# RWKV-6 recurrence and hard-swish MLP on one core: K and R of every chunk on VectorE, chunk 6's keys turned by DMA, and a new order of all steps

## The chip, the cores and the metric

The kernel runs on one core of a Trainium2 chip. The metric is device microseconds of one execution. A core has five engines that each work through a queue of their own, in order: TensorE (PE; its weight loads are shown as PEld), VectorE (DVE), ScalarE (ACT), GpSimd (POOL) and SyncE (SP), which here issues nearly all DMAs. The engines wait for each other through semaphores. An instruction that waits holds up everything behind it in its queue.

## What is computed

The reference, cut to what matters:

```python
# r, k, v, w: (batch 4, heads 8, seq 768, head_dim 48); u: (8, 48)
for t in range(S):
    cur = einsum('bhd,bhe->bhde', u * k[t], v[t])
    y[t] = einsum('bhd,bhde->bhe', r[t], state + cur)
    state = w[t][..., None] * state + einsum('bhd,bhe->bhde', k[t], v[t])
x = y.transpose(0, 2, 1, 3).reshape(3072, 384)
h = x @ w_in                                # w_in (384, 2048), float64
g = h * clip(h + 3, 0, 6) / 6
out = g @ w_out                             # w_out (2048, 384), float64; out is float32
```

So there are 32 recurrences over 768 tokens, and an MLP on their outputs. The MLP's weights come in as 64-bit floats, and the kernel turns them into 32-bit ones itself.

## The kernel before, in words

**Chunks.** The sequence is cut into chunks of 128 tokens, 24 in all, numbered in the order in which they are handled (two sequences run side by side, so chunk i follows chunk i - 2 of its sequence). Each chunk has two halves of 64 tokens. For a chunk i, these steps exist, each with a name that the plan uses:

- `feat` i loads r, k and w by channel (line 356; for chunk 0 in two parts, the second is the step `later`); `tok` i loads v by token (368); `rkt` i loads r and k by token (373). All three are on SP's queue.
- `back` i is a scan over w from behind, on VectorE (434, with a reciprocal at 438), which gives E; `fore` i is a scan from the front (443), which gives W. `K` i multiplies k by E (454), `R` i multiplies r by W in place (458). `least` i keeps the products of a half (461, ScalarE).
- `own` i forms the u sums, that is, for each token and head the sum of r, k and u. For i < `BY_PE` VectorE multiplies r and k by channel (467) and TensorE sums them with u as weights (`dot` i, 16 small products, 479). For later chunks GpSimd multiplies r, k and u by token (470, 471) and VectorE sums (`sum` i, 487). `diag0`/`diag1` i put the sums on the diagonals of the score matrix A (495, ScalarE).
- `score` i forms K times R (504); `above` i copies the part above the diagonal into A (511, VectorE).
- The keys are needed by token as well. For i < `FLIP` TensorE turns them (520, four transposes) and ScalarE copies them out (528). For i >= `FLIP`, `split` i (ScalarE, 537) parts the 32-bit words of K into 16-bit halves, `flip` i (SP, 542) is a DMA that transposes, and `turned` i (ScalarE, 526) puts the halves together.
- `write` forms the chunk's keys times values (620), `kvs` i copies them out (631, ScalarE), and `decay`, `mid`, `decb` and `state` i bring the state on (550 to 566, VectorE).
- `read` i of the chunks from block 1 on is one step on TensorE: read the state (598), form the scores and the key-value products of chunk i + 1 (504, 620), read the values (607), and, where `FLIP` does not apply, turn the keys of chunk i + 2. So `read` i needs K, R and the turned keys of chunk i + 1. `leave` i copies y into the MLP's input (706, ScalarE), and `move` (713, SP) moves the last pair of heads to its place by small DMAs, two times two for a block of four chunks.

**The MLP.** Four chunks make a block (512 tokens), six in all. Block 0's up products (739) are plain, 16 steps of 128 columns (f = 0 to 15), each in two or three parts by chunk (`up0.f.c`), each followed by `ramp` (729, ScalarE) and `gate` (750, VectorE). From block 1 on the up products go by a fast matrix scheme with fewer multiplications (840; 40 steps of four matmul records for a block), with sums of weights ahead (`sin`, 787 to 791, VectorE), sums of x (`tx`, the same lines), and reads of the products (848, 855, 857) before `clip` (861) and `gate` (865). The down products (897; `down` block.half.k.x, eight matmul records each) go by such a scheme too, with sums of g (`sum` block.half.k.x, 882) and of w_out (`sout`, 816).

**The weights.** 16 pieces `fetch` 0 to 15 of 768 KB come in through three buffers (397). Each is converted by ScalarE (`low`, 406, and `sign`, 411) and VectorE (`shift`, 417, and `full`, 421). Later 22 pieces come in once more to be vetted (`refetch`, `vet`, 934 to 952).

**What sets the order.** Every step is entered in a plan with its engine, an estimate of its time, what it follows and which buffers it holds. `Plan.order` (line 191) takes the order itself from a string written out by hand, `ORDER` (82 to 115): two characters give the rank of each step. Each engine's queue is that order, restricted to its steps. The plan's estimates set no order; they only say where TensorE gets dummy products in the first 60 us (`Plan.emit`, 232; `spin`, line 1276), which keep it at work while it has nothing else.

The lines that choose by chunk are few:

```python
448        def early(i):
449            return nc.vector if i < EARLY else nc.gpsimd
454            early(i).tensor_mul(d["K"], d["k"], d["E"][:, :, 1:])
458            early(i).tensor_mul(d["R"], d["r"], d["R"])
465            if i < BY_PE:
531            return i >= FLIP
```

Buffers that matter below: three of `feat` (a load waits until K and R, and with `BY_PE` also `own`, of the chunk three before are done), two of K, two of W, one of `rk` (shared by the u products and the split keys), one of `kvs` (shared by the flipped keys and the copied key-value products), four banks for products.

Of the kernel before, what the change touches and what calls it, by code (L numbers as in the profile page):

```python
# [79 lines left out]

CODE = "ABCDEFGHIJKLMNOPQRSTUVWXYZabcdefghijklmnopqrstuvwxyz0123456789+/"
ORDER = (
    "AEAIAHASATAVAKANAOAPAQARAbAjAXAYAZAaAhApAdAoAyA4A7AGALAeAmAiAsAlAWAcAtAuAvA+BCAwAxA8A9BDBPBHBIBMBdBiAfBhA1BKBNBQA6A2"
    "BEBFBJBpBzB0BLBVBnB1CBCJCLCNCeCkAgBYBTBlB7CKBfBRBoBtB4CaChCnB+CACSCWCMCpCrDYC3C5DTDBBjCOBwCsCqCtB3ByCHCfDJDLDUDfC7DD"
    "DRD0D3EDEIEPEVEzB5EUC6DMDaDgDIDADPDXEEEWEcDcD1EoEKFBFJFaFTFwHZG5CgFSDvECEvExD4ELElEyFPFQFhEhFmFWFrF0F/GmG1EXGUEmFiGD"
    "GRFZFbFjFlFvGHGtGFGMGbGpG9HBHFHKHcHdHfHxFRGfGSGZGzG7GYFnF4F9G6HeHtGkGlGoH9HSH/IBIgI1JqFUHMFVGjGuHjH5GnIXIoI+I/JBG4HY"
    "H7JcJsJtJuJvKkK4LELKHaKaJKH+JUJYKSJNJMJQKBKHLMJfKAKOKlKgKnKvLSLiHbK6HiJZKXK8LGJ5KbKuKzLILXK0K+LHLhLNLtLuLyL2MOL9IUJ+"
    "KeKyLYLkLqLBLmLnLsMBMCLeLfLgMdMeMfMuNQLCL7MRLzMFL5L/L1MjMmMxMyMzMGMUMYM7NCNDNwN3PyPvLdNTL8MpM+M6NZM0MqMrNLNkN5NNNRNn"
    "ONNqOQObOxO+PcM/NEN0NMNWNzOCNPOHOUPDPOPbNXN2OAPaO7PdPfPhPjQDQMQKNSOpOeNxOGPHPNN6PMPsP+P/QCO0PCPERWQ+RXRlRvRyScN1Q0PI"
    "PiP4QAQzP1QyQ3RPRQR2QBQIQnR5RFR7R8SQS/TmUBUCPlRxPwQiQxSASzQsRMRbTCTDTGSBSTSpTfS5TiTjTqT4UMQ4SISKRJSlTPTSRVSnSqTWTXUJ"  # L90
    "S7TITdUGTLUOUSUVUZUaUdUeSVTyTZTATsUDUPTNT+UXUoUpU3TtT6UAVQVRVZVaVdVoWuUQU6URUcUuUrVjUsUmUtUxVsVvU4U5VMVzVbV2WQWhW/Xe"
    "YMX1U0WXVHVIVkWPW+VKVlV7WNWfXFWZWzW0XZWGXbXrX3YJU7VrXaWHW2XTXhWkXfXmXpX2X7XHXOXYX+XMYBYCYWYeYxYjBgAFAJAkAnAqAzBWCTCU"
    "BcCbAMA0A5ArA/BXBZBmBrB2A3BABBBOBUCPCwCxCoDFAAABADACAUBkBvCEB6CRDrD7EOEQEaDCDlDnDwDyETEfEiEkE2E8E9FEE/FFFDFLFMFHFXB8"
    "CdDdC/DiD+EdEeEZErC+DWDjDmD/BSBaBbDpDtDxDqDzD2BGBeBsCCCcCiFAFOFgCjClCuDQDVDZEbEpEwC1C2C8CvCyCzEAEHEJCDCVCZE+FGFIDHDK"
    "DOESEYEnCXCYCmDsD5D6EMENERD9EFEGBqBuBxFpFuGLB/CFCQF7F8GODSDeDhEtE3E4DuD8EBEqEuE0B9CGCIEgEjEsDbDkDoE5E6E7C0C4DEGNGXGc"
    "C9DGDNGdGiGxFeFyF3GPGTGsG8G+HDHEHIHNHOHPHRHTHUHhHkHqHrHzH3H6IAIHIIILIPIeIhIiIkInIrI2I3I4I5I6I7JAFdFfFkFqGVGgF2GBE1GA"
    "FzF+FYGCF1GKFCFKFsFtFcFoF5F6GGGQGIGJGhGqFNFxGEGWGeGaG2HXIEGrHLG/HQGyHgHJHlGwG0GvHAHHHmHGHVHuHvHoHpH0H1G3HCHWHnHwHsH8"
    "IVINHyH2H4IJIKIbIpIyJSIZIlIxICISIsIDIMIYIGITIcIvIwI9IRIdIjIFIqIaImIuIQIOJEI8IWItIfIzI0JHJVJgJhJ0J7JGJXKiKjJkJ6LTLUJC"
    "JDJLJPJFJTJnJ1KKJpJxKCJaJbJ2JJJWJmJRJeJzJ/J4KGJIJlJoJOJrJwJyJ9JiJdKDKLJjKIJ3KJKFKPKQKRKUKhKoKVKWLDLWKEKMKtK/KNKTKsLA"
    "J8K3KfK1KcKdKwK9KZKmKYKpKrLFKxK2LQLRLLLOLZLaKqK5K7LJLvLPLrOfL+LVL4LwL6LjMELxMJLbLlLcLpMHMML3MAMIMNMKMLMbMhLoL0MDMPMa"  # L100
    "MVMkNAOgMQMSMcM8MlMvM3NJNgM5NFNcM4NaNlMTMiMsMWMgMwNGNKNdMtM2NfMZNIM1M9NHMnMXNUNeMoNmNBNbNVNhNjNuOIOLOYNoNyOMOnNYNiPr"
    "PtNONpPJPVN/OFOTOjOvOEOROlODOJOqNsN4N8NrN9OPOdOXOoOBOOOZNtOcOKOWOaN7NvOkOmN+OwOSOhOiOyOzO3O4PnPoOuO2PqP2OtO1PKPkOrOs"
    "P0P5OVO6PFPRO8PBPLPeO5O/O9PGPPPTPQPSPWPgPYPZPxPzPAPUPXP8PpPmQVT7TJP3QUQGQYP6QLQJQpP7P9QFQHQOQRQPQQQlQqQWQXQjQkQNQTQS"
    "QeQ5QhQmQ6SJQZQaQbQcQuQ/RERSRhRCRHRUR+R/ShQdQvQ8QfQwRBRLRGRYQ2RASSQtRRQ9RKRNQ1QgRTRaQ7SoRDRZRORgRqR3SDSCSYRdRkTHTURo"
    "RpTQTRRsR4TnTvRmRzR9SOSgSLSRSmStSuS0RfRnR1RcRtR0SUSPSaRuR6SyRiSNSFSGSZRrReSWSrRwS+SMSbSXSfSjSkSxT2T5S1S2TkTrSiSsTxTz"
    "SdSeTYTgSESHS9TOS3TMTBThSwS4SvS6TTTVTETFTbTuTcTeT3T9S8TKTaTlT1TpT/W7X0TwT0UNUhULUWUYUiUEUFUIUUUTUjUfUgUwU1UlUnUyUzUH"
    "UbUkUqU+UvU/VqWyU8U9VSVpVBVVVhVxWFWdWeWwVNVOVWVAVEVGVCVUVeVuVtV5VLVXVTVDVwVPVgWmVFVJWBWxVYVcVfV4V1V6WbXPXQWJWiX5X6Vn"
    "V3WaWcWIWKXqXyViV0V9WEWYW3XIXAXBXdWTWWWsV8WDWRVyWAWVWnWqW4WCWUWjV/WlWSWpXUWMV+XGXiWOWtWgWoWrW8XkXoYHXCXEYKYXW1W9YDYE"
    "XJXKYIYQWvW5YOYVYYY/YZYkYlYqYPYgYUYiYsYtYoYpZAZCYuYvY7Y9YhY5YrY4ZMY6ZEaFZxW6XVXcXwXLXsXgX4XRXSXWXXXnYFXtXuX8X9YRYSYa"
    "YbXjXlXvYGYmYTYfYwZwZTaEYzY0Y1Y2ZGZPZeZlZzZZZbZkaiala+Y3ZHZNY8ZJZQZiZhZnZKZSa2ZDZfZOZcZdZIZFZrZqZLbYZWZjZmZuZ0Z5aLau"  # L110
    "bAZ8aVbdbfaPaUbQbSZgZ1bHbPZRZ2aIaQagaHaOaXaxa5bRZyZ7Z6ZoaKaRafaYakZaZ4bDZ3aJZ+aNaSZ/Z9aTacaMbbaWahaZanaparasbmbnaeaj"
    "bcbpaoaqa3a/aaabbGbLadazawbEatbFbBbOaya4ama7a8bMa9bCbZbgbVbWbhbia6bUbKbTb8bXbtcEb9cDbubjbobsb+brbybxb1bkbqblbwb2b4bz"
    "b0cAcBb5b/cIcKbvb7b3b6cHcCcMcGcJcFcNQoQrZVZXToUKZpaAYyZBXNYAZUZYX/YcXzYNRIRjPuQEZsaBYnY+aDavT8U2YLYdaCa0ZtZvaGa1VmWL"
    "bIbJXDXxbNbabecL"
)
# [1509 lines left out]
```

## Time and profile before

| | |
|---|---|
| three runs | 526.06, 528.02, 531.23 us; median 528.02 |
| the profiled execution | 528.87 us, of which the span from the first to the last instruction is 527.1 us |
| mean granted TensorE clock | 0.997 |
| ScalarE busy | 290.1 us of the span (55%) |
| K and R on GpSimd (lines 454, 458) | 17 each, 25.0 and 25.3 us busy |
| u products on GpSimd (470, 471) | 15 each, 17.5 and 16.5 us busy |
| TensorE's largest lines | 897 (down) and 840 (up), 29% and 28% of the chain that ended last |
| HBM traffic | 59.69 MB read, 4.72 MB written |

A row of the busy groups names the line, the engine, the operation, what is written from what, and the shapes; then comes the count, the busy time in us, the mean of one in ns, and the idle time of the engine just before, with what ended it. A row of the timeline starts with the start and the time of a run of equal instructions. A row of the chain has only start, time and what. TensorE's instructions overlap in the records: a row's time includes the drain of its last one.

### The profile page before, as it was taken

The page shows a single profiled execution, that of the slowest core. Times are in us where ns is not written, and L with a number is a line of the kernel's source. Part 1 is how long each engine was busy: PE and PEld are TensorE (multiplying, and loading weights), DVE is VectorE, ACT ScalarE, POOL GpSimd, SP SyncE. Part 2 cuts the span into 40 slices and gives each one's busy share as a digit, 9 for nine tenths or more (in the row PEclk, how much of TensorE's full clock was granted, in tenths as well). Part 3 has the DMA queues.
Part 4 walks back from the last instruction along what each step waited for, and adds up shares of the span by engine and source line. Part 5 has one row for each costly group of instructions (what it writes and reads, how often), then busy time and mean ns, then how long its engine had stood idle before and what let it go on. Part 6 is the DMA issues. An engine that isn't in the chain of part 4 may idle for free.

```text
span 527.1 us, 13608 instructions
## 1 busy us (share of the span) xinstructions
PE 517.7 (98%) x5642; PEld 477.7 (91%) x5642; DVE 431.6 (82%) x762; ACT 290.1 (55%) x680; POOL 86.7 (16%) x79
## 2 busy tenths in 40 slices
...
GB/s 329 329 275 182 234 285 92 49 53 181 150 3 63 54 172 68 96 206 72 109 99 101 150 10 130 140 101 106 265 33 153 101 151 203 131 199 136 60 10 57
DMA packets 37235, 70.33 MB, mean 133 GB/s; under 512 B 19088, under 2 KB 27184, under 8 KB 37168
## 3 DMA queue, kind: packets, MB, share of 16 engines
...
q14 instruction: 21, 0.17, 0.1%
q10 hardware_dynamic: 128, 0.00, 0.0%
HBM read 59.69 MB, written 4.72 MB: 122 GB/s over the span
## 4 chain that ended last, share of the span: by engine, by line
PE 86%; DVE 6%; DMA 3%; SPq 2%; ACT 1%; issue 1%; DVEq 0%
PE bank L897 29%; PE bank L840 28%; PE bank L739 8%; PE bankS L897 5%; PE bankS L840 5%; PE y_ps L598 2%; PE bank L504 2%; PE y_ps L607 2%; PE y_ps L620 2%; DMA feat_in<-in_feat_dram 1%; PE bankS L1276 1%; PE ps L479 1%; DMA bits<-in_moe_w_in_dram 1%; SPq L713 1%; DVE E L434 1%
## 5 line engine op out<-in xcount | busy, mean ns | idle before, releaser
L861 ACT ACTIVATE clip<-g,three 128x512 f32<-128x512 f32 x80 | 56.1, 719 | 49.0 <-DVE g L857 27.8
L857 DVE TENSOR_TENSOR g<-bank,g 128x512 f32<-128x512 f32 x80 | 53.4, 684 | 26.2 <-PE bank L840 23.1
L897 PE MATMUL bank<-w_out,g 128*128 128x192 f32 x384 | 67.3, 327 | 0.0
L897 PEld LDWEIGHTS bank<-w_out,g 128*128 128x128 f32 x384 | 63.2, 190 | 0.5
L865 DVE SCALAR_TENSOR_TENSOR g<-clip,g 128x512 f32<-128x512 f32 x80 | 59.1, 754 | 4.0 <-ACT clip L861 3.9
L495 ACT ACTIVATE A<-eyes,dg 128x64 f32<-128x64 f32 x192 | 49.8, 338 | 0.5 <-DVE dg L487 0.3
L454 POOL TENSOR_TENSOR K<-feat_in,E 112x512 f32<-112x512 f32 x17 | 25.0, 1469 | 146.0 <-DVE E L434 82.8
L855 ACT COPY g<-bank 128x512 f32<-128x512 f32 x50 | 28.8, 585 | 33.5 <-PE bank L840 32.3
L739 PE MATMUL bank<-xT,w_in 128*128 128x256 f32 (+1 forms) x216 | 46.7, 366 | 0.0
L739 PEld LDWEIGHTS bank<-xT,w_in 128*128 128x128 f32 x216 | 37.4, 194 | 4.5 <-issue 0.3
L458 POOL TENSOR_TENSOR W<-feat_in,W 112x512 f32<-112x512 f32 x17 | 25.3, 1490 | 94.4 <-DVE W L443 80.9
L840 PE MATMUL bank<-xT,w_in 128*128 128x256 f32 x160 | 40.1, 379 | 0.0
L706 ACT COPY xT<-y_ps 48x256 f32<-48x256 f32 x88 | 32.2, 365 | 10.4 <-PE y_ps L607 9.6
L915 ACT ACTIVATE o<-bank 128x192 f32<-128x192 f32 x36 | 11.5, 327 | 47.1 <-PE bank L897 47.0
L897 PE MATMUL bankS<-w_out,g 128*128 128x192 f32 x192 | 34.9, 328 | 0.0
L897 PE MATMUL bank<-more,g 128*128 128x192 f32 x192 | 34.4, 329 | 0.1
L840 PEld LDWEIGHTS bank<-xT,w_in 128*128 128x128 f32 x160 | 30.2, 190 | 3.8
L897 PEld LDWEIGHTS bank<-more,g 128*128 128x128 f32 x192 | 31.4, 190 | 1.1 <-DVE o L917 0.5
L434 DVE TENSOR_TENSOR_SCAN E<-feat_in,back 112x520 f32<-112x520 f32 x24 | 29.9, 1245 | 2.8 <-DMA feat_in<-in_feat_dram 2.8
L470 POOL TENSOR_TENSOR rk<-rk_in 128x384 f32<-128x384 f32 x15 | 17.5, 1164 | 88.9 <-DMA kvs<-rk 39.4
L897 PEld LDWEIGHTS bankS<-w_out,g 128*128 128x128 f32 x192 | 31.6, 190 | 0.2
L840 PE MATMUL bank<-xT,bits 128*128 128x256 f32 x120 | 30.7, 380 | 0.8 <-DMA xT<-xT 0.8
...
## 6 DMA issues: line engine op xcount, KB each, us to landing
feat_in<-in_feat_dram SPq DMA_DIRECT2D x23, 772.5 KB, 5.7
bits<-in_moe_w_in_dram SPq DMA_DIRECT2D x8, 768.0 KB, 7.3
bits<-in_moe_w_out_dram SPq DMA_DIRECT2D x8, 768.0 KB, 5.6
feat_in<-in_moe_w_in_dram SPq DMA_DIRECT2D x8, 768.0 KB, 4.8
feat_in<-in_moe_w_out_dram SPq DMA_DIRECT2D x8, 768.0 KB, 4.5
...
feat_in<-in_wflat_dram SPq DMA_DIRECT2D x6, 768.0 KB, 4.7
```

What stands on the lines that cost most here:

```text
L434: nc.vector.tensor_tensor_scan(out=E_[:, ::-1], data0=d["w"][:, :0:-1], data1=back.rearrange("q p t -> q (p t)")[:, ::-1], initial=0.0, op ...
L454: early(i).tensor_mul(d["K"], d["k"], d["E"][:, :, 1:])
L458: early(i).tensor_mul(d["R"], d["r"], d["R"])
L495: nc.scalar.activation(out=d["A"][:, h, :], in_=eyes, func=ACT.Copy, scale=d["dg"][:, h])
L706: nc.scalar.copy(out=blocks[bk]["xT"][g * GP:g * GP + D, :, at:at + HL], in_=st[i]["y_ps"][a][(g ^ a) * GP:(g ^ a) * GP + D, :, :])
L739: nc.tensor.matmul(h_ps[:, :(c1 - c0) * L], lhsT=w_in[:, f // 2, j, f % 2, :], rhs=b["xT"][:, j, c0 * L:c1 * L], start=(j == 0), stop=(j = ...
L840: nc.tensor.matmul(b["p", d, c][:, z * HB:(z + 1) * HB], lhsT=weight(W_PLACE[r], d)[:, z, :], rhs=x_at(bk, X_PLACE[r]), start=fresh and z ...
L855: nc.scalar.copy(out=out_, in_=src)
L857: nc.vector.tensor_tensor(out=out_, in0=src, in1=out_of(bk, d, other), op=ALU.add if sign > 0 else ALU.subtract)
L861: nc.scalar.activation(out=c, in_=out_of(bk, d, u), func=ACT.Relu, bias=three, scale=twice)
L865: nc.vector.scalar_tensor_tensor(out=g, in0=blocks[bk]["r", d, u], scalar=6.0, in1=g, op0=ALU.min, op1=ALU.mult)
L897: nc.tensor.matmul(b["d", p, to][:, :h], lhsT=a, rhs=w(), start=(f == 0 and k in (1, 5)), stop=(f == HF - 1 and k in (2, 3, 4)), skip_grou ...
```

## The change

Three constants and the order string change; no function does.

```diff
-BY_PE = 9
-FLIP = 7
+BY_PE = 8
+FLIP = 6
 OWN = -16.106
 SOLO = (0, 1, 2, 3, 4)
-EARLY = 7
+EARLY = 24
...
 ORDER = (
-    "AEAIAHASATAVAKANAOAPAQARAbAjAXAYAZAaAhApAdAoAyA4A7AGALAeAmAiAsAlAWAcAtAuAvA+BCAwAxA8A9BDBPBHBIBMBdBiAfBhA1BKBNBQA6A2"
+    "AAAKABAHAIAUAEAFAGAMANAOAWAfAPAQAXAcAgAqAnAsA0A6BFADAiAVAhAeApAZARASAYAaAmAxAzAkAuAyA7A8BQBGBHBKBXBYALA5AwBCBABLA/Aj"
...
```

- `EARLY` 24: `K` and `R` of chunks 7 to 23, 34 steps, are formed by VectorE and no longer by GpSimd.
- `BY_PE` 8: chunk 8's u sums are formed as those of the later chunks. `dot8` (TensorE) goes, `own8` moves from VectorE to GpSimd, `sum8` from ScalarE to VectorE, and the load `rkt8` comes. GpSimd is left with the u products of chunks 8 to 23.
- `FLIP` 6: chunk 6's keys are turned by DMA. The four transposes in `read4` go, `split6` (ScalarE) and `flip6` (SP) come, and `turned6` becomes the longer copy.
- All 1808 steps (1806 before) stand in a new order.

Read out, the order begins so on SP's queue (before, then after):

```
fetch6 feat0 later feat1 tok0 fetch0 tok1 fetch2 feat2 feat3 fetch4 fetch1 fetch3 tok3 u tok2 feat4 fetch7 feat5
feat0 later feat1 fetch1 tok0 feat2 fetch3 tok1 fetch0 feat3 tok3 tok2 fetch2 fetch6 feat4 fetch7 feat5
```

On TensorE at the start:

```
dot0 turn0 kv0 score0 dot1 clear0 first0 turn1 read0 kv1 score1 dot2 up0.1.0 clear1 first1 turn2 up0.0.0 read1 kv2 dot3 up0.8.0 score2
dot0 turn0 dot1 score0 kv0 turn1 clear0 first0 score1 kv1 dot2 read0 clear1 first1 turn2 read1 score2 dot3 kv2 up0.0.0 up0.1.1 turn3
```

On VectorE at the start:

```
shift6 back0 own0 K0 fore0 full6 R0 own1 back1 decb0 fore1 above0 K1 state0 shift0 shift2 R1 full0 back2
back0 own0 K0 fore0 own1 R0 back1 shift1 fore1 above0 decb0 K1 own2 R1 state0 full1 shift3 back2
```

On ScalarE, the conversions (`low` and `sign`) ahead of `leave1` are those of pieces 6, 0, 2 and 4, with `low3`, before, and of 1, 3 and 0 after.

On TensorE between chunk 4's read and chunk 5's, after: `up0.3.0 dot6 up0.11.0 up0.2.0 up0.9.2 up0.11.2 up0.14.2 up0.3.2 dot7 up0.15.2 up0.13.2 up0.7.2 up0.2.2 up0.6.2`.

On TensorE from chunk 6's read to block 1:

```
read6 down0.0.4.1 down0.1.5.0 down0.1.1.0 down0.1.1.1 down0.1.5.1 down0.1.6.0 down0.1.2.0 down0.1.6.1 read7 down0.1.2.1 down0.1.7.0 down0.1.7.1 down0.1.3.0 down0.1.3.1 down0.1.4.0 down0.1.4.1 up1.0.12 up1.0.1
read6 down0.0.4.0 down0.0.4.1 down0.1.5.0 down0.1.5.1 read7 down0.1.6.0 down0.1.6.1 down0.1.2.1 down0.1.7.0 down0.1.7.1 down0.1.3.0 down0.1.3.1 down0.1.4.0 down0.1.4.1 up1.0.1 up1.0.12
```

Ahead of `read6` stand, after: `down0.0.3.0 down0.0.3.1 down0.0.7.0 down0.0.7.1 down0.1.2.0`; VectorE has `out0.0.c12 R7 K8 sum0.1.1.0 out0.0.c22 sout4.0` in that stretch, the first of which follows `down0.0.3.1`.

On SP around chunk 7's way out:

```
flip9 move1.0.0 feat10 feat11 move1.1.0 rkt11 move1.1.1 store0.1 store0.3
move1.0.0 feat9 store0.1 feat10 feat11 move1.1.0 move1.1.1 flip9 store0.2
```

(`move1.0` is block 1's first pair of chunks, 4 and 5; `move1.1` its second, 6 and 7.)

More of the change, by code (lines that the diff above doesn't have):

```diff
@@ L112 @@
-    "bcbpaoaqa3a/aaabbGbLadazawbEatbFbBbOaya4ama7a8bMa9bCbZbgbVbWbhbia6bUbKbTb8bXbtcEb9cDbubjbobsb+brbybxb1bkbqblbwb2b4bz"
-    "b0cAcBb5b/cIcKbvb7b3b6cHcCcMcGcJcFcNQoQrZVZXToUKZpaAYyZBXNYAZUZYX/YcXzYNRIRjPuQEZsaBYnY+aDavT8U2YLYdaCa0ZtZvaGa1VmWL"
-    "bIbJXDXxbNbabecL"
+    "AAAKABAHAIAUAEAFAGAMANAOAWAfAPAQAXAcAgAqAnAsA0A6BFADAiAVAhAeApAZARASAYAaAmAxAzAkAuAyA7A8BQBGBHBKBXBYALA5AwBCBABLA/Aj"
+    "A2A9BDBUBaBhBJBVBdBnBBBoBsB6CZCgA3A4BEBgCGCUBWBZBbBfB1CLCcClBmB0B7CHB4ChCnDSCrC7DeDgBPDECACVC9DbCKB3CFCJC1DODcDpC0C+"
```

58 lines of the change are left out of this document (30 added, 28 removed).

## The prediction, made before the changed kernel ran

> **What bounds the kernel now.** I read the page's totals first, then the chain that ended last, then the busy time by stretches of 30 us.
>
> ```profile
> span 527.1 us, 13608 instructions
> PE 517.7 (98%) x5642; PEld 477.7 (91%) x5642; DVE 431.6 (82%) x762; ACT 290.1 (55%) x680; POOL 86.7 (16%) x79
> PE 86%; DVE 6%; DMA 3%; SPq 2%; ACT 1%; issue 1%; DVEq 0%
> 0.00:30.00 30.00, 26.42 (x440) 24.59 (x440) 25.90 (x47) 21.99 (x58) 3.01 (x15) 1.00 0.87 330
> 60.00:90.00 30.00, 30.00 (x416) 26.34 (x416) 29.45 (x59) 24.93 (x57) 1.18 (x1) 1.00 0.66 227
> 90.00:120.00 30.00, 30.00 (x305) 28.55 (x304) 29.07 (x52) 15.00 (x39) 5.65 (x4) 1.00 0.19 47
> 150.00:180.00 30.00, 30.00 (x376) 27.34 (x371) 29.14 (x53) 20.55 (x45) 5.57 (x4) 1.00 0.14 36
> 270.00:300.00 30.00, 30.00 (x294) 28.92 (x293) 20.37 (x39) 11.88 (x31) 6.75 (x6) 1.00 0.29 82
> ```
>
> A stretch shows its length, then PE, PEld, DVE, ACT, POOL, the clock, DMA share and GB/s. TensorE is busy throughout and makes 86% of the last chain; GpSimd makes none of it. So the relief of GpSimd is worth nothing by itself: only less TensorE work, or an earlier or less broken supply of it, moves the end. VectorE is the second engine, nearly full in 60 to 120 and 150 to 180, with room later (20.37 of 30). Where does TensorE still lose time? In two places.
>
> The first is the start. TensorE is filled there with dummy products (line 1276), and real work waits for data.
>
> ```profile
> L1276 PE MATMUL bankS<-ident 128*128 128x128 f32 x94 | 15.6, 328 | 1.4 <-POOL ident masks.py:199 1.4
> 9.99 2.02 PE bankS L1276 x18
> 5.66 0.56 DVE L417 TENSOR_SCALAR top<-bits 128x768 int32<-128x768 int32 x1 [2.30 <-DMA bits<-in_moe_w_in_dram]
> 6.21 1.24 DVE L434 TENSOR_TENSOR_SCAN E<-feat_in,back 112x520 f32<-112x520 f32 x1
> 33.03 1.24 DVE L434 TENSOR_TENSOR_SCAN E<-feat_in,back 112x520 f32<-112x520 f32 x1 [2.19 <-DMA feat_in<-in_feat_dram]
> ```
>
> 18 dummies in 2.02 us are 0.112 us each, so 94 fill 10.5 us. The scan at 33.03 is chunk 4's and waits 2.19 us for its load: the start is fed by a DMA stream that runs flat out (330 GB/s over 0 to 30).
>
> The second is the step from block 0 to block 1.
>
> ```profile
> 122.42 1.51 ACT L706 COPY xT<-y_ps 48x256 f32<-48x256 f32 x4 [1.64 <-PE y_ps L607]
> 124.58 1.79 SPq L713 DMA_DIRECT2D xT<-xT  x3
> 126.41 0.58 SPq L373 DMA_DIRECT2D rk_in<-in_tok_dram  x1
> 127.10 1.77 SPq L713 DMA_DIRECT2D xT<-xT  x3
> 128.92 2.76 PE L897 MATMUL bank<-more,g 128*128 128x192 f32 x16
> 132.52 1.10 PE L840 MATMUL bank<-xT,bits 128*128 128x256 f32 x4 [0.84 <-DMA xT<-xT]
> 132.83 0.43 DVE L787 SCALAR_TENSOR_TENSOR T__1844<-xT 128x256 f32<-128x256 f32 x1 [3.36 <-DMA out_dram<-o]
> 134.78 1.10 PE L840 MATMUL bank<-T__1844,bits 128*128 128x256 f32 x4 [1.16 <-DVE T__1844 L787]
> 91.23 2.60 PE bank L897 x16
> 161.57 5.18 PE bank L840 x24
> ```
>
> Chunk 7's output is copied out until 123.93, its moves land only at about 132.5, and the x sums start at 132.83. Sixteen down products take 2.60 us in the chain (0.1625 each, 1.30 for a step of eight, which I call a half), so those of 128.92 are issued by 131.5; the first up product starts at 132.52, and the second at 134.78, where 0.86 after the first would do (24 in 5.18 us, 0.216 each, four to a step). That is 1.0 + 1.4 = 2.4 us lost.
>
> **The change part by part.** *K and R of chunks 7 to 23 on VectorE.* 34 instructions leave GpSimd and join VectorE's queue.
>
> ```profile
> L454 POOL TENSOR_TENSOR K<-feat_in,E x17: 1172/1627/1711, 73.6 to 393.4; 112x512 f32<-112x512 f32 x17
> L454 DVE TENSOR_TENSOR K<-feat_in,E x7: 682/685/687, 8.2 to 66.0; 112x512 f32<-112x512 f32 x7
> 109.17 1.40 DVE L791 TENSOR_TENSOR bits<-w_in 128x256 f32<-128x256 f32 x1
> 113.36 0.40 DVE L791 TENSOR_TENSOR bits<-w_in,bits 128x256 f32<-128x256 f32 x1
> L857 DVE TENSOR_TENSOR g<-bank,g 128x512 f32<-128x512 f32 x80 | 53.4, 684 | 26.2 <-PE bank L840 23.1
> L865 DVE SCALAR_TENSOR_TENSOR g<-clip,g 128x512 f32<-128x512 f32 x80 | 59.1, 754 | 4.0 <-ACT clip L861 3.9
> ```
>
> VectorE takes on 34 x 0.685 = 23.3 us. It gives up a stretch: the sum at 109.17, beside a K on GpSimd, took 1.40 instead of 0.40, and the gate of line 865 (both inputs in SBUF) means 754 ns against 684 for the read of line 857, of the same size with one input in PSUM. From the gates alone that is 80 x 0.07 = 5.6 us, which includes GpSimd's u products; at most it is 34 x 1.0. Adding over all VectorE groups what an instruction took beyond its group's median gives 21 us, of which about 16 lie under a K or R. Net load on VectorE: +7, between -11 and +23. On the path I take 0: TensorE's queue has its next products ready in these stretches. If that cover goes, it costs rival two.
>
> *Chunk 8's u sum to GpSimd, chunk 6's keys by DMA.* TensorE loses 16 + 4 instructions.
>
> ```profile
> 40.26 0.56 PE ps L479 x16
> 36.60 0.39 PE ps L520 x4
> L537 ACT COPY rk<-K 112x1024 uint16<-112x1024 uint16 x17 | 17.7, 1040 | 2.0 <-POOL K L454 1.9
> DMA to landing us min/median/max: 2.9/3.1/4.6
> L526 ACT COPY kn<-kvs 128x896 uint16<-128x896 uint16 x17 | 20.4, 1198 | 9.2 <-DMA kvs<-rk 9.2
> ```
>
> That is 0.56 + 0.39, and all of it is on the path: -0.95 us. SP gets one more load (rkt8) and one more flip, ScalarE a split and a longer copy; the split, the flip's 3.1 to landing (the quoted row is that of line 542, the flip) and the copy are 5.3 us behind K6. Between chunk 4's read and chunk 5's, which needs the turned key, the new order has twelve up steps (ten of six 256-wide products at 0.216, 1.3 us; two half as wide) and two u dots of 0.56, some 15 us, so it is hidden (without that cover: up to 5.3).
>
> The Trainium skill speaks against this edit: "VectorE: DVE Perf Modes", section "The three transpose paths", gives TensorE 390 ns and the DMA path 1309 ns for one 128x128 tile. The rows here agree on the order (0.39 us for four tiles against 3.1 to landing). By that rule the edit would add latency, up to +5.3; by the chain, where only TensorE's time counts, it saves 0.39.
>
> *The new order, at the start.* SP's list now begins with chunk 0's and 1's loads and puts five weight pieces ahead of chunk 4's, not six.
>
> ```profile
> feat_in<-in_feat_dram SPq DMA_DIRECT2D x23, 772.5 KB, 5.7
> bits<-in_moe_w_in_dram SPq DMA_DIRECT2D x8, 768.0 KB, 7.3
> L411 ACT ACTIVATE more<-bits 128x768 bf16<-128x768 int32 x16 | 17.1, 1071 | 0.0
> L406 ACT ACTIVATE more<-bits 128x768 uint16<-128x768 uint32 x16 | 17.2, 1077 | 3.8 <-DMA bits<-in_moe_w_in_dram 3.1 <-DVE w_out L421 0.7
> ```
>
> 768 KB less ahead of chunk 4 (the 16 pieces are alike) are 0.786 MB, or 2.4 us at 330 GB/s. On ScalarE one weight conversion (1.077 + 1.071 = 2.15 us) fewer stands ahead of chunk 1's way out (three where there were four), and the first scan need not follow a weight piece (back0 at 6.21 waited behind 5.66 + 0.56; up to 0.7). Against it, chunk 1's turn on TensorE now stands ahead of chunk 0's read and waits for K1, which VectorE forms only after chunk 0's mask copy: about 0.6 later there. Three ways of looking give 0 (if the three weight buffers hold SP's queue, whose later pieces wait for conversions), 2.15 and 2.4. I take -2.2. The bounds: -4.5, if a fair part of the 10.5 us of dummies goes; +1.5, if chunk 0's detour is not made up.
>
> The granted clock rides on this stretch too: six products took 2.59 us at 31.89 where six take 1.46 at 89.77.
>
> ```profile
> 31.89 2.59 PE L739 MATMUL bank<-xT,w_in 128*128 128x256 f32 x6
> 89.77 1.46 PE L739 MATMUL bank<-xT,w_in 128*128 128x256 f32 x6
> ```
>
> That is 1.1 us. The Trainium skill, "TensorE: Matmul & The Clock Gate", Part 1, has the clock fall after an idle window of about 3.4 us that runs free of the program; by it this 1.1 us may go or stay whatever the order, so the sum counts nothing where the row alone would let me take it.
>
> *The new order, at block 1.* Two down halves move from ahead of chunk 7's read to behind it: nine (11.7 us at 1.30) now cover the way from that read to the first up product, where there were seven. In SP's list no load stands between the four moves any more, where rk_in stood with 0.58. That would erase the 2.4. But chunk 7's read now comes four halves (5.2 us) after chunk 6's, where it came after eight. It needs chunk 8's turned key and chunk 7's state: from K8, which VectorE forms three down steps ahead of chunk 6's read, split 1.04, flip 3.1 to 4.6, copy 1.2 and chunk 6's way out (as chunk 7's, 1.5) make 6.8 to 8.3 us, against seven halves, 9.1, and the read between them. So it is just hidden, and a late K8 shows at once. I take -1.8, from -2.4 to +2.
>
> *Everything else.* The later reads are moved by a few products each way; between two of them stand seven halves or as much in up steps, 9.1 us, or more. Nothing there is idle to be won; small new waits may come: +0.5, from 0 to 4.
>
> Sum: -0.95 - 2.2 - 1.8 + 0.5 = -4.45. The profiled execution took 528.87 (its span 527.1 and 1.77 around it), so 524.4. It lies 0.85 above the median of the three runs, 528.02; on their scale, 523.5.
>
> **The rivals.** *One: the start gains more.* If TensorE gets its first long run of products as much earlier as chunk 4's load arrives (2.4) and part of the dummies beyond (4.5 in all), and block 1's 2.4 goes whole: -0.95 - 4.5 - 2.4 = -7.85, and on the scale of the median 520.2. For it: the start is the one place with real slack; against: only three weight pieces can lie unconverted, and ScalarE is at 21.99 of 30 already.
>
> *Two: slower, VectorE becomes the bound.* Place: the in-order queue of VectorE in each of the five blocks from chunk 5's read on. Price: 23.3 us joins it, and only the 5.6 that the gates show comes back; 17.7, of which the stretches with room take a half, leave 9, with TensorE's -0.95 and the start's -2.2 some +6: 534. It decides as soon as a block's stretch has less than some 4 us of 30 free; 60 to 120 and 150 to 180 have under 1. Against it: most other stretches are like 270 to 300, and the stretched sums show that much more than 5.6 comes back.
>
> *Three: nothing but a trade.* Block 1's wait moves to chunk 7's read (a flip of 4.6 or a late K8: +2 in place of -1.8), and the start gives 0: -0.95 + 2 + 0.5 = +1.55, 529.6. For it: the 5.2 us between two reads, the shortest of either order; against: K8 no longer takes GpSimd's 1.6 us.
>
> **How the numbers follow.** My forecast, a gain of 2 to 6.5 us, 0.60; rival one 0.17; rival three 0.15; rival two 0.08. One per cent is 5.28 us, about what a measurement of this kernel tells from no change. Of the forecast's cases nearly half lie beyond it (0.25 of 0.60), and all of rival one's: faster 0.42. Rival two gives slower, 0.08; the rest, 0.50, lies within. The forecast's own range is 521.5 to 526; with rival one and half of rival three, 519 to 528.5.
>
> **What would show it right or wrong.** Right: GpSimd at about 35 us busy (86.7 less 34 at 1.6, and one more u product pair) with only lines 470 and 471 at work; VectorE at 430 to 445 with line 865 back at about 700 ns; chunk 4's scan at about 30 instead of 33.03, and fewer than 94 dummies or an earlier end of them; no wait at block 1's first up products; TensorE's stretches from 150 on as full as before. Wrong: a stall of 2 us or more in front of chunk 7's read (line 598, near 120); line 454 or 458 as releaser of TensorE; VectorE over 29 of 30 in several stretches beyond 180; six 256-wide products of line 739 not seen before 31.89.

## The result, and the profile after

The changed kernel took 521.65 us (median of six runs, 521.15 to 523.82), the kernel before beside it 527.43 (six runs, 526.06 to 531.23). The ratio is 0.9872, with a 95% interval of 0.9844 to 0.99: faster by 1.3%. The profiled execution took 522.23, its span 6.7 us less than before.

The page of the changed kernel: totals, engines, the chain, and two groups of instructions.

```profile
span 520.4 us, 13521 instructions
...
PE 511.6 (98%) x5608; PEld 474.1 (91%) x5608; DVE 434.8 (84%) x796; ACT 292.5 (56%) x680; POOL 39.4 (8%) x47
...
PE 91%; DMA 3%; DVE 2%; ACT 1%; SPq 1%; issue 1%; DVEq 0%
...
L865 DVE SCALAR_TENSOR_TENSOR g<-clip,g 128x512 f32<-128x512 f32 x80 | 53.5, 684 | 6.6 <-ACT clip L861 6.4
...
L470 POOL TENSOR_TENSOR rk<-rk_in 128x384 f32<-128x384 f32 x16 | 19.0, 1187 | 361.4 <-DMA kvs<-rk 111.8
```

TensorE has a larger share of the chain (91% for 86%), VectorE a smaller one (2% for 6%). GpSimd has lost 47 us, and line 865 takes 684 ns where it took 754. VectorE took on 23.3 us of K and R and is busy only 3.2 us longer: its instructions beyond their groups' medians summed to 21.3 us before and to 3.0 now.

By stretches of 30 us (length, then PE, PEld, DVE, ACT, POOL, clock, DMA share, GB/s):

```profile
0.00:30.00 30.00, 27.56 (x493) 25.44 (x494) 26.94 (x51) 22.14 (x62) 3.01 (x15) 1.00 0.90 341
...
60.00:90.00 30.00, 30.00 (x420) 26.82 (x420) 28.19 (x58) 25.51 (x57) 2.00 (x2) 1.00 0.47 156
90.00:120.00 30.00, 29.36 (x413) 28.53 (x412) 29.03 (x58) 14.23 (x39) 0.00 (x0) 1.00 0.38 115
```

VectorE is still nearly full from 60 to 120 (28.19 and 29.03 of 30). The timeline at the start shows chunk 0's scan, chunk 0's read, chunk 1's read, chunk 3's scan and chunk 4's scan:

```profile
3.90 1.24 DVE L434 TENSOR_TENSOR_SCAN E<-feat_in,back 112x520 f32<-112x520 f32 x1 [0.53 <-DMA feat_in<-in_feat_dram]
...
15.43 0.65 PE L598 MATMUL y_ps<-W,S 48*48 48x64 f32 x16
...
20.65 0.65 PE L598 MATMUL bank<-W,S 48*48 48x64 f32 x16
...
21.35 1.24 DVE L434 TENSOR_TENSOR_SCAN E<-feat_in,back 112x520 f32<-112x520 f32 x1
...
32.90 1.24 DVE L434 TENSOR_TENSOR_SCAN E<-feat_in,back 112x520 f32<-112x520 f32 x1
```

The same of before, where the forecast did not show them:

```profile
16.12 0.65 PE L598 MATMUL y_ps<-W,S 48*48 48x64 f32 x16
...
24.35 0.65 PE L598 MATMUL bank<-W,S 48*48 48x64 f32 x16
...
26.60 1.23 DVE L434 TENSOR_TENSOR_SCAN E<-feat_in,back 112x520 f32<-112x520 f32 x1
```

The first scan comes 2.3 us earlier (3.90 for 6.21), chunk 3's 5.25, chunk 1's read 3.7. Chunk 4's scan is where it was (32.90 for 33.03), now with no wait for its load. And at the step to block 1:

```profile
113.05 0.67 PE L598 MATMUL y_ps<-W,S 48*48 48x64 f32 x32 [0.64 <-ACT xT L706]
...
116.30 4.05 SPq L713 DMA_DIRECT2D xT<-xT  x6
...
123.08 0.42 DVE L787 SCALAR_TENSOR_TENSOR T__1814<-xT 128x256 f32<-128x256 f32 x1 [0.49 <-DMA xT<-xT]
...
126.83 1.03 PE L840 MATMUL bank<-T__1814,bits 128*128 128x256 f32 x4
```

No wait stands at the first up products any more; chunk 7's read waits 0.64 us for chunk 6's way out.

To say where the time went, I set against each moment the real TensorE work issued until then: dummies count nothing, an up product of line 840 its 0.216 us, a down product its 0.1625, a 128-wide product of line 739 0.112, the small ones of reads and u sums 0.007 to 0.03, each an issue interval from an undisturbed row. Time passed less this work is **lost TensorE time**. For the two kernels, and for five of the experiments below:

| us lost by | 60 | 100 | 110 | 120 | 140 | 200 | 300 | 515 |
|---|---|---|---|---|---|---|---|---|
| before | 27.1 | 29.9 | 30.8 | 31.0 | 34.5 | 37.8 | 41.9 | 49.3 |
| after | 23.2 | 25.7 | 26.4 | 28.1 | 28.0 | 31.6 | 35.9 | 43.6 |
| K and R alone | 27.1 | 29.7 | 30.6 | 30.8 | 33.2 | 38.5 | 45.4 | 58.2 |
| new order to chunk 8's read | 23.4 | 25.7 | 26.6 | 27.5 | 27.3 | 31.2 | 35.0 | 42.1 |
| new start alone | 21.6 | 25.3 | 32.2 | 32.5 | 33.8 | 37.4 | 41.3 | 48.3 |
| new start, seam mended | 24.5 | 28.6 | 31.6 | 33.1 | 36.4 | 39.2 | 43.9 | 50.9 |
| before, moves first | 27.6 | 30.5 | 31.1 | 31.5 | 32.3 | 35.9 | 40.2 | 47.6 |

The gain of after: 3.9 us up to 60, 0.5 from 60 to 110 (3.2 lost for 3.7), 2.1 from 110 to 140 (1.6 for 3.7); 0.8 is lost again behind that (15.6 for 14.8), and the work itself is 0.8 smaller (473.7 for 474.5). That makes 6.5 of the span's 6.7.

### The profile page after: what moved, and what is told of

Its sections match the earlier page's. It is cut to its first block, busy times and chain, and to the rows that moved or that the text cites. A ratio compares the mean times of both kernels' runs of the same rounds, so it can differ in the third digit from the quotient of the medians.

```text
span 520.4 us, 13521 instructions
## 1 busy us (share of the span) xinstructions
PE 511.6 (98%) x5608; PEld 474.1 (91%) x5608; DVE 434.8 (84%) x796; ACT 292.5 (56%) x680; POOL 39.4 (8%) x47
## 4 chain that ended last, share of the span: by engine, by line
PE 91%; DMA 3%; DVE 2%; ACT 1%; SPq 1%; issue 1%; DVEq 0%
PE bank L897 33%; PE bank L840 28%; PE bank L739 8%; PE bankS L840 5%; PE bankS L897 5%; PE y_ps L598 3%; DMA xT<-xT 2%; PE y_ps L607 2%; PE bank L504 2%; PE y_ps L620 2%; SPq L713 1%; PE bankS L1276 1%; PE ps L479 1%; ACT xT L706 1%; DMA feat_in<-in_feat_dram 1%
## 5 line engine op out<-in xcount | busy, mean ns | idle before, releaser
L861 ACT ACTIVATE clip<-g,three 128x512 f32<-128x512 f32 x80 | 56.4, 719 | 33.8 <-DVE g L857 25.8
L865 DVE SCALAR_TENSOR_TENSOR g<-clip,g 128x512 f32<-128x512 f32 x80 | 53.5, 684 | 6.6 <-ACT clip L861 6.4
L739 PE MATMUL bank<-xT,w_in 128*128 128x256 f32 (+1 forms) x216 | 45.2, 361 | 1.2 <-DMA xT<-xT 1.2
L470 POOL TENSOR_TENSOR rk<-rk_in 128x384 f32<-128x384 f32 x16 | 19.0, 1187 | 361.4 <-DMA kvs<-rk 111.8
L855 ACT COPY g<-bank 128x512 f32<-128x512 f32 x50 | 28.2, 586 | 28.3 <-PE bank L840 25.5
L897 PE MATMUL bank<-more,g 128*128 128x192 f32 x192 | 34.5, 328 | 0.5 <-DVE o L917 0.5
L897 PEld LDWEIGHTS bank<-more,g 128*128 128x128 f32 x192 | 31.6, 190 | 1.1 <-DVE o L917 0.7
L526 ACT COPY kn<-kvs 128x896 uint16<-128x896 uint16 x18 | 21.6, 1201 | 15.8 <-DMA kvs<-rk 7.8
L443 DVE TENSOR_TENSOR_SCAN W<-feat_in,start 112x520 f32<-112x520 f32 x24 | 29.6, 1233 | 0.0
```

The costliest lines, as they stand in the source:

```text
L443: nc.vector.tensor_tensor_scan(out=W_, data0=d["w"][:, :-1], data1=starts[i % 2].rearrange("q p t -> q (p t)"), initial=0.0, op0=ALU.mult, ...
L526: nc.scalar.copy(out=d["kn"].bitcast(U16).rearrange("q p (d two) -> q two p d", two=2), in_=d["flip"])
L739: nc.tensor.matmul(h_ps[:, :(c1 - c0) * L], lhsT=w_in[:, f // 2, j, f % 2, :], rhs=b["xT"][:, j, c0 * L:c1 * L], start=(j == 0), stop=(j = ...
L855: nc.scalar.copy(out=out_, in_=src)
L861: nc.scalar.activation(out=c, in_=out_of(bk, d, u), func=ACT.Relu, bias=three, scale=twice)
L865: nc.vector.scalar_tensor_tensor(out=g, in0=blocks[bk]["r", d, u], scalar=6.0, in1=g, op0=ALU.min, op1=ALU.mult)
```

## The experiments

Each ratio is against the kernel before, run beside it on the same chip, with its 95% interval. The experiments ran on two chips at four times, and the kernel before took 527.98 to 528.73 us beside them (527.43 beside the changed kernel), so differences of a microsecond between two variants are not settled by their times alone.

### K and R on VectorE, by themselves

In the order of before (first), and taken out of the changed kernel (second):

```diff
-EARLY = 7      # K and R alone: the kernel before, and only this
+EARLY = 24
```
```diff
-EARLY = 24     # the changed kernel with K and R on GpSimd
+EARLY = 7
```

> The kernel before with one constant changed: K and R of chunks 7 to 23 on VectorE, the old order kept. Theory A (TensorE bounds; the gain lies in the order, at the start and at block 1): K and R on VectorE are worth nothing by themselves, 526.5 to 528.5 beside 527.4 of before. Theory B (K and R off GpSimd are the gain: no stretched sums, no wait for GpSimd): 524 or less, at least 3 us of the 5.8. Theory C (VectorE overloaded in 60 to 120 where it stood at 29 of 30 us): 529 or more, with new waits before line 598 or 840.

> The changed kernel with K and R of chunks 7 to 23 back on GpSimd, the new order kept. Theory A: the start and its 4 us stay, chunk 7's read waits some 1 to 2 us more for K8 and R8; 522 to 524.5. Theory B: the gain goes, 526 or more. If the order is made for K and R on VectorE (the two belong together): VectorE's queue waits for GpSimd in many places, over 527.

K and R alone: **536.19** against 527.98, 1.0173 [1.0136, 1.0209], slower by 8.2 us. The changed kernel with K and R on GpSimd: **521.61**, 0.9881 [0.9857, 0.9906], the changed kernel's own time, and a little under the 522 at which its expectation began. So the edit is worth nothing in the new order and costs 1.7% in the old one. The page of the second kernel shows GpSimd at work again, at no cost in time:

```profile
PE 514.0 (99%) x5608; PEld 476.1 (92%) x5608; DVE 430.4 (83%) x762; ACT 292.7 (56%) x680; POOL 89.1 (17%) x81
...
L865 DVE SCALAR_TENSOR_TENSOR g<-clip,g 128x512 f32<-128x512 f32 x80 | 57.1, 730 | 5.1 <-ACT clip L861 4.9
```

GpSimd is busy 89.1 us, line 865 is stretched to 730 ns, and the time is the same. K and R alone has the sign of theory C, but not its place. Its loss is not VectorE's load (438.2 us, 82% of its span; the changed kernel has 434.8, 84%, and no loss) but the order of VectorE's queue. The timeline near 412, at its longest wait:

```profile
411.91 0.68 DVE L865 SCALAR_TENSOR_TENSOR g<-clip,g 128x512 f32<-128x512 f32 x1
412.51 0.69 DVE L458 TENSOR_TENSOR W<-feat_in,W 112x512 f32<-112x512 f32 x1
...
413.34 0.69 PE L504 MATMUL bank<-W,K 48*64 48x64 f32 x32 [2.15 <-DVE W L458]
```

R stands at a place that was planned for GpSimd, where it had no gates ahead of it (there it ran at 397.80 in the kernel before); here it comes behind them, and TensorE waits 2.15 us for R. Its clock falls behind that, as the stretches of this kernel show:

```profile
411.00:414.50 3.50, 1.35 (x87) 1.25 (x81) 3.22 (x7) 2.87 (x4) 0.00 (x0) 1.00 0.19 19
414.50:418.00 3.50, 3.50 (x32) 2.79 (x22) 3.46 (x8) 0.05 (x1) 0.00 (x0) 0.53 1.37 245
```

Until 140 us this kernel is no worse than before (33.2 lost for 34.5); it loses from 180 on. The other waits there are shorter, 0.2 to 0.8 us each, for results of VectorE (lines 550, 787, 857, 917) and of ScalarE (526, 706, 915).

### Where in the order the gain lies

The steps are kept; two orders are joined at a read. K and R of chunks 7 to 23 are on GpSimd in both of these.

```diff
 order of the steps:
-as changed
+as before up to chunk 8's read, then as changed        (later part alone; BY_PE 9, FLIP 7)
+as changed up to chunk 8's read, then as before        (new order to chunk 8's read; BY_PE 8, FLIP 6)
```

> All constants as before; the old order up to chunk 8's read, the new order after it, K and R on GpSimd. By the theory that the gain ends with block 1's start: 527 to 528.5, as before. If the later blocks have a share: 526 or less.

> As the start-only kernel, but with the new order kept up to chunk 8's read, past block 1's start. If block 1's step gives 1.6 net beside the start: 521 to 522, as the changed kernel, and 1 to 2 us under the start-only kernel. If the step gives nothing net (its 2.4 us went to chunk 7's read): the same as the start-only kernel.

The later part alone: **529.04** against 528.08, 1.0023 [1.0, 1.0046]. The new order up to chunk 8's read: **521.03**, 0.9863 [0.9833, 0.9893]. All of the gain lies ahead of 140 us; the order of the four later blocks is worth nothing, and so is K and R on VectorE there.

Two earlier tries at this cut had K and R on VectorE in the old part too, or chunk 6's turn at a place of my choice in it, and both lost more than they were to show:

```diff
+as changed up to chunk 5's read, then as before        (EARLY 24)
+as before up to chunk 8's read, then as changed        (EARLY 24, BY_PE 8, FLIP 6)
```

> The three constants of the change; the new order up to chunk 5's read, the old one for all steps after it. Theory A, by the lost TensorE time added up in both profiles (27.0 us against 23.0 at 60 us): the start alone gives 4.0, and TensorE's 20 fewer products 0.7: 522.5 to 524, with block 1's wait of about 2 us still there. If the rest of the order made the gain instead: 526 or more.

> The three constants of the change; the old order up to chunk 8's read, the new one for all steps after it. Theory A: nothing is won behind block 1's start, so what stays is TensorE's 0.7: 526 to 527.5. If the new order of the later blocks has a share: 525 or less.

**535.35** and **537.22** against 527.98, 1.0155 [1.0124, 1.0187] and 1.0192 [1.0156, 1.0228]. The first has the loss of K and R alone in its old part, and near 105 us that of the new start alone, shown below. The second is a case of its own: chunk 6's turned key came to stand on ScalarE ahead of the activations of the up products.

```profile
81.29 1.19 ACT L526 COPY kn<-kvs 128x896 uint16<-128x896 uint16 x1 [3.10 <-DMA kvs<-rk]
...
84.22 6.95 PE L739 MATMUL bank<-xT,w_in 128*128 128x256 f32 x18 [5.62 <-DVE g L750]
```

ScalarE waits 3.10 us for the DMA's transpose, and TensorE 5.62 for what is queued behind it; TensorE's clock is 0.51 from 83.0 to 90.0. This is the price of this edit without its cover. The forecast gave it as up to 5.3, which the wait alone exceeds, and left the clock out. It says nothing against the changed order, which has the cover, and neither run divides the gain.

### The start

One weight piece first again, as in the order of before (SP's load, with its conversions on ScalarE and VectorE first too), in the changed kernel:

```diff
-feat0 later feat1 fetch1 tok0 feat2 fetch3 tok1 fetch0 feat3 tok3 tok2 fetch2 fetch6
+fetch6 feat0 later feat1 fetch1 tok0 feat2 fetch3 tok1 fetch0 feat3 tok3 tok2 fetch2
```

> The changed kernel, with weight piece 6 loaded ahead of chunk 0 and converted ahead of it on ScalarE and VectorE, as the order before has it; all else of the new order stays. If the start's gain is that chunk 0's and 1's data come and are worked on ahead of weights: chunk 0's scan at about 6.2 instead of 3.9, chunk 1's read 1.5 to 2.5 later, 523 to 524. If the gain comes from where TensorE's steps stand: 521.5 to 522.3.

**523.45** against 528.08, 0.9913 [0.9879, 0.9948]: 1.8 us over the changed kernel (the intervals still overlap). Chunk 0's scan starts at 6.23, as expected, and chunk 1's read at 23.32, 2.7 us later than in the changed kernel; 94 dummies run again for 80, and 25.0 us are lost by 60.

And the new start alone: the changed order up to chunk 5's read, the old one behind it, K and R on GpSimd.

```diff
+as changed up to chunk 5's read, then as before        (EARLY 7, BY_PE 8, FLIP 6)
```

> K and R of chunks 7 to 23 on GpSimd as before; chunk 6 flipped and chunk 8's u sums on GpSimd as in the change; the new order up to chunk 5's read, the old order after it. So nothing but the start is new. If the start gives 4.0 and the fewer products 0.7: 522.5 to 523.5 beside 527.5 to 528 of before, with block 1's wait of about 2.4 us still in the trace. If the first run of this kind lost its gain to the start itself and not to K and R in the old order: 527 or more.

**528.12** against 528.08, 1.0001 [0.9981, 1.002]: no gain, though by 60 us it is 5.5 ahead of before. The table shows where the lead goes: 6.9 us are lost between 100 and 110. Its timeline there:

```profile
100.99 1.10 DVE L791 TENSOR_TENSOR bits<-bits,w_in 128x256 f32<-128x256 f32 x1
101.78 1.35 POOL L454 TENSOR_TENSOR K<-feat_in,E 112x512 f32<-112x512 f32 x1
102.02 1.93 DVE L816 TENSOR_TENSOR more<-w_out,top 128x768 f32<-128x768 f32 x1
103.87 0.61 DVE L917 SCALAR_TENSOR_TENSOR o<-bank,o 128x192 f32<-128x192 f32 x2
...
104.27 2.93 PE L897 MATMUL bank<-more,g 128*128 128x192 f32 x8 [3.30 <-DVE o L917]
```

The next down step needs the bank that line 917 empties, and line 917 stands in VectorE's queue behind a scan and two sums, which R and K on GpSimd stretch besides (1.10 and 1.93, elsewhere 0.42 and 0.95). In the kernel before the same queue reaches line 917 later still, and nobody waits, because TensorE comes later too:

```profile
105.50 0.34 DVE L917 SCALAR_TENSOR_TENSOR o<-bank,o 128x192 f32<-128x192 f32 x1
...
106.11 1.46 PE L897 MATMUL bank<-more,g 128*128 128x192 f32 x8
```

VectorE is full there (3.46 of 3.50 from 99.5 on, in the first row below), so a lead of TensorE alone runs into VectorE's queue. Then the clock falls:

```profile
99.50:103.00 3.50, 1.47 (x9) 1.18 (x8) 3.46 (x5) 1.30 (x2) 3.50 (x2) 1.00 0.26 67
103.00:106.50 3.50, 2.23 (x7) 2.23 (x8) 3.50 (x5) 1.04 (x1) 0.13 (x1) 0.54 0.32 61
106.50:110.00 3.50, 3.50 (x118) 3.06 (x120) 1.85 (x6) 0.20 (x1) 0.67 (x1) 0.50 0.09 19
```

The half clock adds to the loss in this execution (526.90), but the loss does not need it: two of the twelve runs have a mean clock of 1.0 and took 527.40 and 528.53.

To test that reading I moved only VectorE's queue at this seam (K8, on GpSimd here, follows chunk 8's scan):

```diff
 sum0.0.4.1
-sin0.3 back8 sin0.4 sout4.0 out0.0.c22 out0.0.c12 sout4.1
+sout4.0 out0.0.c22 sout4.1 sin0.3 out0.0.c12 back8 sin0.4
```

> The kernel with the new order up to chunk 4's and 5's reads and the old order behind them (528.12 against 528.08), with four VectorE steps moved ahead in VectorE's queue near 100 us: the two output sums of line 917 and the two weight sums of line 816 that a down step waits for now stand ahead of chunk 8's scan, its reciprocal, K8 and one up-weight sum. Theory A: the start's lead of some 4 us was lost there because TensorE, 4 us early, found VectorE still busy with a queue planned for the later time (the wait of 3.30 us on line 917 and the half clock for 6.8 us behind it). Then the wait shrinks to under 1 us, the half clock goes, and the time is 523.5 to 525.5. Theory B (rival): the lead is lost because VectorE's total work up to block 1 is full, whatever its order; then the wait moves to the next VectorE result within some 10 us, and the time stays at 527 to 529.

**526.80** against 528.73, 0.9964 [0.9935, 0.9993], a time between the two theories' (the kept trace is of an execution of 529.86). Theory A's wait is gone: from 100.03 to chunk 6's read at 105.44 TensorE waits for nothing. But a next wait came at 106.5, for chunk 7's turned key, followed by half a clock for 3.4 us from 109.8. ScalarE's timeline there, and two waits of TensorE in this kernel (in total, times, longest):

```profile
107.10 0.20 ACT L461 COPY w_min<-E 112x8 f32<-112x8 f32 x1 [6.51 <-DVE E L434]
107.21 1.19 ACT L526 COPY kn<-kvs 128x896 uint16<-128x896 uint16 x1
...
PE y_ps L620 <- ACT kn L526: 1.8, 1, 1.8
PE bank L840 <- DVE T__1830 L787: 1.1, 1, 1.1
```

That wait comes from the edit itself. Chunk 8's scan starts at 105.84 (at 99.60 without the edit, in a trace that is 3.2 us ahead here), ScalarE's copy from it (line 461) waits 6.51 us for it, and chunk 7's turned key stands behind that copy in ScalarE's queue. So the stall was the queue's order, as A says, and one move in VectorE's queue brought another stall through ScalarE's; how much of the lead both queues, mended together, would keep is open. The new order between chunk 5's read and chunk 8's (79 to 143 us) carries the lead through, as the kernel with the new order up to chunk 8's read shows. That VectorE's whole load would forbid it, as B says, is refuted by that kernel.

### The step to block 1

In the changed kernel, chunk 7's read goes behind the two down halves that the change had moved behind it, and its way out follows it; seven halves are the cover, as before the change. Only TensorE's queue is edited.

```diff
-read7 down0.1.6.0 down0.1.6.1 down0.1.2.1
+down0.1.6.0 down0.1.6.1 read7 down0.1.2.1
```

> The changed kernel with chunk 7's read and its way out put behind the two down halves that the change had moved behind them, so that seven halves again cover the way from that read to block 1's first up product. Forecast's reading of block 1: the cover of 2.6 us is what took the wait away, so 1.4 to 2.4 us of wait come back at lines 840 and 787, less the 0.64 that chunk 7's read now waits: 522.5 to 523.5. Rival: the wait went because no load stands between the four moves any more and the lead of the start reaches VectorE, not by the two halves: 521.0 to 521.7, no wait at the first up products.

**522.98** against 528.73, 0.9892 [0.9856, 0.9929], 1.3 us over the changed kernel, with overlapping intervals. It lies in the forecast's range, but not for the forecast's reason: no wait came back at the first up products. TensorE waits for VectorE's g sums instead, because the two halves are asked for a read earlier, and once for ScalarE's copy of an output (line 915). The trace is of the slowest of the six runs, 524.21.

```profile
PE bank L897 <- DVE S__1535 L882: 1.6, 2, 1.2
PE bank L897 <- ACT o L915: 0.5, 1, 0.5
```
```profile
119.34 1.51 ACT L706 COPY xT<-y_ps 48x256 f32<-48x256 f32 x4 [3.79 <-PE y_ps L607]
...
126.35 0.42 DVE L787 SCALAR_TENSOR_TENSOR T__1814<-xT 128x256 f32<-128x256 f32 x1 [1.42 <-DMA xT<-xT]
...
129.17 1.03 PE L840 MATMUL bank<-T__1814,bits 128*128 128x256 f32 x4
```

From the start of chunk 7's way out to the first x sum are 7.0 us here; before, from 122.42 to 132.83, they were 10.4, with the same seven halves. The moves' view says why. Before, first for all nine moves from 120 us on, then for the six of chunk 7 that stand behind the loads; then here:

```profile
DMA to landing us min/median/max: 1.8/4.9/6.7
```
```profile
DMA to landing us min/median/max: 4.5/5.6/6.7
```
```profile
DMA to landing us min/median/max: 1.8/2.2/3.3
```

Before, chunk 7's moves were issued right behind two chunk loads and around a third load, and their landing took 5.6 us in the median instead of 2.2. Here, SP issued the chunk loads at 111.96, 8.5 us ahead of the moves; in the changed kernel itself, at 111.67, 4.6 us ahead, and the median landing is 3.1. The start of the loads in the timeline of before:

```profile
122.70 1.79 SPq L356 DMA_DIRECT2D feat_in<-in_feat_dram  x2
```

So I made one more edit, in the kernel before and on SP alone:

```diff
-move1.0.0 feat10 feat11 move1.1.0 rkt11 move1.1.1 store0.1
+move1.0.0 move1.1.0 move1.1.1 feat10 feat11 rkt11 store0.1
```

> The kernel before with one edit in SP's list: the loads of chunk 10 and 11 and chunk 11's keys and values stand behind the last moves of chunk 7's output, not ahead of and between them. Nothing else is moved, so seven down halves still cover the way from chunk 7's read to block 1's first up product. Theory A: block 1's wait of 2.0 to 2.4 us in the kernel before came from the loads' transfers, which filled the DMA engines while the moves were in them (moves took 4.9 us from issue to landing there, 2.2 in the changed kernel with seven halves); then the moves land in about 2 to 3 us, the first up products wait under 0.5 us, and the time is 525.7 to 527. Theory B, the forecast's: seven halves are too little cover and the load costs only its 0.58 us of issue; then 1.4 us or more of wait stay and the time is 527.2 to 528.2. If the later loads themselves come too late, a new wait on chunk 10's scan shows near 140 us in either case.

**526.32** against 528.49, 0.9959 [0.9942, 0.9976]: 2.2 us for three loads put behind the moves of one pair of chunks. The timeline:

```profile
129.94 0.41 DVE L787 SCALAR_TENSOR_TENSOR T__1844<-xT 128x256 f32<-128x256 f32 x1
...
132.07 1.03 PE L840 MATMUL bank<-xT,bits 128*128 128x256 f32 x4
132.93 1.03 PE L840 MATMUL bank<-T__1844,bits 128*128 128x256 f32 x4
```
```profile
DMA to landing us min/median/max: 1.8/1.8/2.8
```

The landing is 1.8 us, the x sums come 2.9 earlier (only 0.5 of it because the last move is issued earlier, at 127.8 for 128.3), both waits are gone, and 0.8 us are lost from 120 to 140 for 3.5. Theory A holds, the forecast's cover does not decide. The Trainium skill, "DMA: Bandwidth & Descriptors", section "Two DMAs through the same engine are not ordered", has the descriptors of one queue start in order on an engine, pipelined; these rows agree, since small moves behind 772 KB loads came late, and ahead of them did not.

### Two mends of the changed kernel

Chunk 6's way out ahead of chunk 8's turned key on ScalarE (for the 0.64 at chunk 7's read), and two moves ahead of a load on SP, for a new wait of the changed kernel at the start:

```profile
56.08 2.18 PE L739 MATMUL bank<-xT,w_in 128*128 128x256 f32 x9 [1.17 <-DMA xT<-xT]
```

```diff
-split8 flip8 turned8 above7 ... leave6
+split8 flip8 leave6 turned8 above7 ...
-move0.1.0 feat6 move0.1.1
+move0.1.0 move0.1.1 feat6
```

> The changed kernel with two mends of waits that its trace shows: chunk 6's way out on ScalarE (line 706) ahead of chunk 8's turned key (line 526), so that chunk 7's read no longer waits 0.64 us for it, and the two moves of chunk 2's and 3's output at 48 to 51 us ahead of chunk 6's load on SP, so that the up products at 56.08 no longer wait 1.17 us. Theory A: both waits are on the path: 521.65 - 0.6 - 1.2 = 519.9. Theory B: what is won early is taken back by the next wait (turned8 comes 1.5 us later, feat6 0.9 later): 521.2 to 522.2.

**520.79** (519.78 to 521.58) against 528.73, 0.985 [0.9813, 0.9887]. Both waits are gone:

```profile
54.40 5.36 PE L739 MATMUL bank<-xT,w_in 128*128 128x256 f32 x24
...
111.74 1.01 PE L598 MATMUL y_ps<-W,S 48*48 48x64 f32 x30
```

The trace loses 42.1 us in all for 43.6, the medians differ by 0.86, and the intervals of the two ratios overlap: it lies between A and B, and against the changed kernel the gain is not settled. Its median is the lowest of all, but only 0.24 under that of the new order to chunk 8's read.

## Why the prediction was right or wrong

The forecast was 523.5, a gain of 4.5, the range 519 to 528.5; 521.65 lies in the range, 1.85 below the forecast, and the gain is past the 1% that it put at 0.42.

- **"Only less TensorE work, or an earlier or less broken supply of it, moves the end": right.** GpSimd's 50 us back on it cost nothing.
- **K and R on VectorE at 0: right in size, and with a condition that the forecast did not name.** It argued with TensorE's queue having products ready. What makes it so is the new order, in which every K and R has a new place in VectorE's queue; in the old order the price was 8.2. Rival two had nearly this figure (+6) for the wrong reason: it priced VectorE's load in full stretches, and the loss came from places in the queue, from 180 us on, an R behind gates (2.15 us) the longest of several waits. The stretch that comes back was 18 us (21.3 to 3.0), as argued from the gates and sums.
- **The start, -2.2 (bounds -4.5 to +1.5): too small, and at the wrong transfer.** Up to 60 us, the five traces with the old start lose 26.2 to 28.3, the seven with the new one, not mended, 21.6 to 24.5; the means differ by 3.7. The forecast took the gain from chunk 4's load, and put its scan at about 30; it stayed at 32.90. What came earlier is what the forecast gave "up to 0.7": the first scan, 2.3 us, and with it chunks 0 to 3. That the lead lasts only with the new order between chunk 5's read and chunk 8's behind it was not in the forecast at all. The forecast also misread its own row of the dummies: the 94 fill 15.6 us, not 10.5, since up to 6.9 us they stand 0.21 us apart.
- **The clock's 1.1 us, left out of the sum: here it went with the order.** The old starts show the low period in four of five traces (in one of them at 8.6), the new ones never; the one old start without it loses 26.2, so some 2.8 of the 3.7 are left without the clock. The runs' mean clocks agree: 48 of the 68 runs of the kernel before that stand beside the experiments lie under 0.999, and none of the 30 of the changed kernel and the four variants that keep its order up to chunk 8's read, but for small moves. Beside each experiment, the median of those runs of before that reach 0.999 is 1.0 to 1.5 us lower than that of all. So about 1 us of the gain seems to be a low clock that no longer comes, and "may go or stay whatever the order" did not hold in these runs.
- **Block 1, -1.8: right in size (2.1 from 110 to 140), wrong in cause, so the size was luck.** "Nine now cover the way, where there were seven" failed: seven suffice, and the wait came from loads in the DMA engines, priced in the forecast at SP's issue time of 0.58. The fear that chunk 7's read, 5.2 us behind chunk 6's, waits for the turned key did not come true; it waited 0.64 for ScalarE.
- **TensorE's 20 products, -0.95:** 0.8 in the sum of real work. No run takes it apart from the order.
- **Chunk 6's key by DMA:** hidden, as said. The latency of the DMA path shows only where the cover is gone, in the 3.10 and 5.62 us above.
- **New waits, +0.5 (0 to 4):** 1.17 and 0.64 in the trace, 0.8 lost in the later blocks.

What the forecast named as marks came out: GpSimd at 39.4 (for about 35) with line 470 and its pair 471, VectorE at 434.8, line 865 at 684, 80 dummies, no wait at the first up products, stretches behind nearly as full (none under 29.4 of 30). Only chunk 4's scan did not. Rival one's 4.5 for the start is nearer to the 3.7, the forecast's 2.2 to the 2.8 without the clock; the time fell between the two.

Open: which of the loads behind the first piece bring the rest of the start's gain, and why the start varies by 2.9 us between traces of the same order (21.6 to 24.5). The variation goes along with the time up to which the dummies stand 0.21 us apart instead of 0.112: 4.3 us in the trace that loses 21.6, 10.8 in the one that loses 24.5. No run changes that time by itself.
